# A GeGLU feed-forward kernel on one core: the first token block is transposed by DMA in 128-row slices, all its tiles accumulate at once, and two weight chunks run on it before block two

## The chip, the cores and the metric

The kernel runs on one core of one Trainium2 chip. The metric is device time in microseconds (us), as a median over executions. The profile's span is about 2 us shorter than the device time (590.8 us for a run of 592.9 us).

## The reference

```python
B, S, D, F = 1, 2048, 1024, 3584           # all bf16
def reference(x, w_gate, w_up, w_down):
    return (gelu_tanh(x @ w_gate) * (x @ w_up)) @ w_down
```

The three products are 2688 matmuls of 128x128 weights on 512 columns.

## The kernel before

The 2048 tokens are worked in two halves. A half has two token blocks of 512. Gate and up weights come in seven chunks of 512 columns (1 MB each for gate and up), two chunks in memory at a time. The contraction over D=1024 has eight k-slices of 128. TensorE needs x with D on the partitions (xT), so x must be transposed. Only the start of the first half matters here. Block one comes in two pieces of 512 KB and is transposed by TensorE; three gate and three up tiles (six PSUM banks) accumulate side by side as slices arrive:

```python
    NSU = 3; NWARM = 9; WKP = 2
    load_x0_piece(0, nc.sync)          # xs0[:, :, 0:512], plain load
    load_w0_piece(0, nc.scalar)        # k-slices 0,1 of gate and up, 256 KB each
    ...                                # 9 warm-up matmuls on a constant
    for wp in range(1, NWP):           # the rest of chunk 0, with x piece 1 between
        load_w0_piece(wp, nc.sync)
    for tb in range(1, NTB):           # block two: one 1 MB DMA transpose
        nc.sync.dma_start_transpose(out=xT[:, :, 512:1024], in_=xv[512:1024, :, :])
    chunk_tiles[1] = load_chunk(1)
    # [cut: 7 loads of w_down, 1 MB each]

    def startup_units(hT, wg_sb, wu_sb):
        groups = [transpose_x_piece(0)]          # 16 TensorE transposes + copies
        for kd in range(KD):
            # second transpose_x_piece before kd == 3   [cut]
            g = [mm_gu(su_ps[u][0], wg_sb, xT, u, 0, kd) for u in range(NSU)]
            g += [mm_gu(su_ps[u][1], wu_sb, xT, u, 0, kd) for u in range(NSU)]
    # afterwards: fg (chunk) outer, tb (block) inner
```

The framework that issues the DMAs owns eight completion semaphores for the queues of SP and ACT. It hands them out in the order in which it schedules the DMAs, over both queues. A ninth DMA reuses the first one's semaphore, and its issue waits until that first DMA has landed.

Of the kernel before, what the change touches and what calls it, by code (L numbers as in the profile page):

```python
# [7 lines left out]

ACT = mybir.ActivationFunctionType
ALU = mybir.AluOpType  # L10
BF16 = mybir.dt.bfloat16
# [7 lines left out]
def kernel(  # L19
# [8 lines left out]
    nc = tc.nc  # L28
    P = 128
    x2 = x.flatten_outer_dims()  # L30
# [5 lines left out]
    TB = 512  # L36
# [7 lines left out]
    NDN = D // DN  # L44
    NTS = SH // P
    TSB = TB // P
    XQ = min(512, D)
    NXQ = D // XQ
    KPQ = XQ // P
    WKP = 2 if KD % 2 == 0 else 1  # L50
    NWP = KD // WKP
    NSU = min(3, FPG)
    NWARM = 9

    xv = x2.rearrange("t (ko ki) -> t ko ki", ki=P)
    wgv = w_gate.rearrange("(ko ki) f -> ki ko f", ki=P)
    wuv = w_up.rearrange("(ko ki) f -> ki ko f", ki=P)
    wdv = w_down.rearrange("(ko ki) d -> ki ko d", ki=P)

    const_pool = ctx.enter_context(tc.tile_pool(name="const", bufs=1))  # L60
    xT_pool = ctx.enter_context(tc.tile_pool(name="xT", bufs=1))
    xs_pool = ctx.enter_context(tc.tile_pool(name="xs", bufs=1))
    hT_pool = ctx.enter_context(tc.tile_pool(name="hT", bufs=1))
    wd_pool = ctx.enter_context(tc.tile_pool(name="wd", bufs=1))
    wgu_pool = ctx.enter_context(tc.tile_pool(name="wgu", bufs=2))
    g_pool = ctx.enter_context(tc.tile_pool(name="g", bufs=3))
    o_pool = ctx.enter_context(tc.tile_pool(name="o", bufs=3))
    psum = ctx.enter_context(
        tc.tile_pool(name="psum", bufs=8, space=bass.MemoryType.PSUM)
# [2 lines left out]
    def ps_tile(name):  # L72
        return psum.tile([P, TB], F32, name=name, tag="ps")

    wd_sb = wd_pool.tile([P, KF, D], BF16, name="wd_sb")

    xs0 = xs_pool.tile([P, TSB, D], BF16, name="xs")
    xT = xT_pool.tile([P, KD, SH], BF16, name="xT")
    wg0 = wgu_pool.tile([P, KD, FG], BF16, name="wg_sb")
    wu0 = wgu_pool.tile([P, KD, FG], BF16, name="wu_sb")  # L80

    def load_x0_piece(q, eng):
        eng.dma_start(
            out=xs0[:, :, q * XQ : (q + 1) * XQ],
            in_=x2[0:TB, q * XQ : (q + 1) * XQ].rearrange("(ts p) d -> p ts d", p=P),
        )

    def load_w0_piece(wp, eng):
        k0, k1 = wp * WKP, (wp + 1) * WKP
        eng.dma_start(out=wg0[:, k0:k1, :], in_=wgv[:, k0:k1, 0:FG])  # L90
        eng.dma_start(out=wu0[:, k0:k1, :], in_=wuv[:, k0:k1, 0:FG])

    load_x0_piece(0, nc.sync)
    load_w0_piece(0, nc.scalar)

    nc.scalar.preload_act_table(ACT.Gelu_apprx_tanh)  # L96

    ident = const_pool.tile([P, P], BF16, name="ident")
    make_identity(nc, ident[:])

    warm_insts = []
    if NWARM > 0:
        warm_l = nc.const_aps.tensor(1.0, [P, P], BF16)
        warm_r = nc.const_aps.tensor(1.0, [P, TB], BF16)
        warm_ps = ps_tile("warm_ps")
        for i in range(NWARM):
            warm_insts.append(
                nc.tensor.matmul(  # L108
                    warm_ps[:], lhsT=warm_l, rhs=warm_r, start=True, stop=True
                )  # L110
            )

    x_after = {}
    for q in range(1, NXQ):
        wq = min(max((q * KPQ) // WKP - 1, 0), NWP - 1)
        x_after.setdefault(wq, []).append(q)
    for q in x_after.get(0, []):
        load_x0_piece(q, nc.sync)
    for wp in range(1, NWP):
        load_w0_piece(wp, nc.sync)  # L120
        for q in x_after.get(wp, []):
            load_x0_piece(q, nc.sync)
    for tb in range(1, NTB):
        nc.sync.dma_start_transpose(
            out=xT[:, :, tb * TB : (tb + 1) * TB],
            in_=xv[tb * TB : (tb + 1) * TB, :, :],
        )

    chunk_tiles = {0: (wg0, wu0)}

    def load_chunk(fg):
        wg_sb = wgu_pool.tile([P, KD, FG], BF16, name="wg_sb")
        wu_sb = wgu_pool.tile([P, KD, FG], BF16, name="wu_sb")
        nc.sync.dma_start(out=wg_sb[:], in_=wgv[:, :, fg * FG : (fg + 1) * FG])
        nc.sync.dma_start(out=wu_sb[:], in_=wuv[:, :, fg * FG : (fg + 1) * FG])
        return wg_sb, wu_sb

    if NFG > 1:
        chunk_tiles[1] = load_chunk(1)

    WDP = 4
    for k0 in range(0, KF, WDP):
        k1 = min(KF, k0 + WDP)
        nc.sync.dma_start(out=wd_sb[:, k0:k1, :], in_=wdv[:, k0:k1, :])

    evac_ctr = [0]

    def evac(dst, src):
        if evac_ctr[0] % 2 == 0:
            nc.vector.tensor_copy(out=dst, in_=src)  # L150
        else:
            nc.scalar.copy(out=dst, in_=src)  # L152
        evac_ctr[0] += 1

    def transpose_x_piece(q):
        kds = list(range(q * KPQ, (q + 1) * KPQ))
        banks = []
        if q == 0:
            if TSB % 2 == 0:
                banks.append(([kds[0]], (0, TSB // 2)))  # L160
                banks.append(([kds[0]], (TSB // 2, TSB)))
            else:
                banks.append(([kds[0]], (0, TSB)))
            rest = kds[1:]
            if rest:
                banks.append(([rest[0]], (0, TSB)))
                rest = rest[1:]
        else:
            rest = kds
        for i in range(0, len(rest), 2):  # L170
            banks.append((rest[i : i + 2], (0, TSB)))
        pe_insts = []
        for kd_list, (ts0, ts1) in banks:
            n = (ts1 - ts0) * P
            tp = psum.tile([P, len(kd_list), n], BF16, name="tp", tag="ps")
            for j, kd in enumerate(kd_list):
                for ts in range(ts0, ts1):
                    pe_insts.append(
                        nc.tensor.transpose(  # L179
                            tp[:, j, (ts - ts0) * P : (ts - ts0 + 1) * P],  # L180
                            xs0[:, ts, kd * P : (kd + 1) * P],
                            ident[:],
                        )
                    )
            k0 = kd_list[0]
            evac(xT[:, k0 : k0 + len(kd_list), ts0 * P : ts1 * P], tp[:])
        return pe_insts

    def mm_gu(ps, w_sb, xT_, fi, tb, kd):
        return nc.tensor.matmul(  # L190
            ps[:],
            lhsT=w_sb[:, kd, fi * P : (fi + 1) * P],
            rhs=xT_[:, kd, tb * TB : (tb + 1) * TB],
            start=(kd == 0),
            stop=(kd == KD - 1),
        )

    def unit_tail(hT, gate_ps, up_ps, fc, tb):
        g_sb = g_pool.tile([P, TB], F32, name="g_sb")
        nc.scalar.activation(out=g_sb[:], in_=gate_ps[:], func=ACT.Gelu_apprx_tanh)  # L200
        nc.vector.tensor_tensor(  # L201
            out=hT[:, fc, tb * TB : (tb + 1) * TB],
            in0=g_sb[:],
            in1=up_ps[:],
            op=ALU.mult,
        )

    def unit(hT, xT_, wg_sb, wu_sb, fi, fc, tb):
        gate_ps = ps_tile("gate_ps")
        up_ps = ps_tile("up_ps")  # L210
        for kd in range(KD):
            mm_gu(gate_ps, wg_sb, xT_, fi, tb, kd)
        for kd in range(KD):
            mm_gu(up_ps, wu_sb, xT_, fi, tb, kd)
        unit_tail(hT, gate_ps, up_ps, fc, tb)

    def startup_units(hT, wg_sb, wu_sb):
        groups = [transpose_x_piece(0)]
        su_ps = [(ps_tile("gate_ps"), ps_tile("up_ps")) for _ in range(NSU)]
        for kd in range(KD):  # L220
            for q in range(1, NXQ):
                if kd == q * KPQ - 1:
                    groups.append(transpose_x_piece(q))
            g = [mm_gu(su_ps[u][0], wg_sb, xT, u, 0, kd) for u in range(NSU)]
            g += [mm_gu(su_ps[u][1], wu_sb, xT, u, 0, kd) for u in range(NSU)]
            groups.append(g)
        if warm_insts:
            groups.insert(0, warm_insts)
        for ga, gb in zip(groups[:-1], groups[1:]):
            tc.add_manual_dep(  # L230
                gb[0].ins, ga[-1].ins.name, SCHED_DEP, reason="startup PE order"
            )
        for u in range(NSU):
            unit_tail(hT, su_ps[u][0], su_ps[u][1], u, 0)

    for h in range(NH):
        if h > 0:
            xT = xT_pool.tile([P, KD, SH], BF16, name="xT")
            for tb in range(NTB):
                t0 = h * SH + tb * TB  # L240
                nc.sync.dma_start_transpose(
                    out=xT[:, :, tb * TB : (tb + 1) * TB],
                    in_=xv[t0 : t0 + TB, :, :],
                )
        hT = hT_pool.tile([P, KF, SH], BF16, name="hT")
        for fg in range(NFG):
            if h == 0 and fg in chunk_tiles:
                wg_sb, wu_sb = chunk_tiles[fg]
            else:
                wg_sb, wu_sb = load_chunk(fg)  # L250
            for tb in range(NTB):
                fi_start = 0
                if h == 0 and fg == 0 and tb == 0:
                    startup_units(hT, wg_sb, wu_sb)
                    fi_start = NSU
                for fi in range(fi_start, FPG):
                    fc = fg * FPG + fi
                    unit(hT, xT, wg_sb, wu_sb, fi, fc, tb)
        for ts in range(NTS):
            last = h == NH - 1 and ts == NTS - 1  # L260
            o_sb = o_pool.tile([P, D], BF16, name="o_sb")
# [78 lines left out]
```

## Time and profile before

| what | before | where it is read |
|---|---|---|
| device time, first three runs | 592.93 us (592.72 to 594.9) | run times |
| span; TensorE busy | 590.8 us; 586.4 us (99%) | the page, part 1 |
| eight 512-column matmuls | 1.73 us, 0.216 us each | the chain |
| useful work, 2688 x 0.216 | 580.6 us | worked out |
| first x piece landed; first transpose | 5.42; 5.47 us | the chain |
| first matmul after the startup units | 17.83 us, with 48 useful matmuls done | the timeline |
| useful work starts effectively at | 17.83 - 48 x 0.216 = 7.46 us | worked out |

"Effective start" is the measure used throughout: the time at which the first matmul after the first group begins, less the time that the useful matmuls before it need at full speed. Whatever delays the start is in it once, and the kernel's end moves with it.

From the page of the kernel before, parts 1 and 4:

```profile
span 590.8 us, 6172 instructions
PE 586.4 (99%) x2757; PEld 268.6 (45%) x2757; DVE 78.7 (13%) x116; ACT 88.9 (15%) x148; POOL 0.7 (0%) x6
...
PE 99%; DMA 1%; ACT 0%; issue 0%
```

The chain of waits of its first 20 us (start, duration, what; in these views PE is TensorE, PEld its weight loads, and SPq and ACTq are the DMA queues of SP and ACT):

```profile
0.74 4.69 DMA xs<-in_x_dram
5.42 0.05 issue
5.47 1.07 PE tp L179 x16
6.54 0.65 PE gate_ps L190 x3
7.18 0.03 issue
7.22 0.82 PE up_ps L190 x3
...
10.63 0.89 PE tp L179 x16
...
18.00 1.73 PE gate_ps L190 x8
```

### The profile page before, as it was taken

The numbers are of one execution on the slowest core, as the hardware profiler recorded it, in microseconds if no ns is written. First come the engines' busy times: TensorE is split into PE (matmuls) and PEld (weight loads), VectorE is DVE, ScalarE is ACT, GpSimd is POOL, SyncE is SP. The second block draws the span as 40 slices with busy tenths as digits, with TensorE's granted clock in tenths as the row PEclk, the third lists the DMA queues.
The fourth block names the chain that finished last, engine by engine and source line by source line (L and its number), as shares of the span: only waits on it lengthen the run. The fifth ranks groups of instructions, "written<-read, shape, count | busy, mean of one in ns | idle before, by whom it ended". The sixth has DMA issues, their size and how long they took to land.

```text
span 590.8 us, 6172 instructions
## 1 busy us (share of the span) xinstructions
PE 586.4 (99%) x2757; PEld 268.6 (45%) x2757; DVE 78.7 (13%) x116; ACT 88.9 (15%) x148; POOL 0.7 (0%) x6
## 2 busy tenths in 40 slices
PE   8999999999999999999999999999999999999997
PEld 4444444444444444444444444444444444444445
DVE  0211211121122100000011221121122110000000
ACT  2211112111111110101011112111111110101010
POOL 0000000000000000000000000000000000000000
PEclk9999999999999999999999999999999999999999
DMA  9991404041231480000000413214040000000001
GB/s 273 358 378 59 143 0 143 8 136 52 92 99 44 127 176 19 24 31 18 19 18 3 140 41 103 85 58 131 12 143 1 0 1 0 24 30 19 18 19 36
DMA packets 48969, 45.47 MB, mean 77 GB/s; under 512 B 13360, under 2 KB 43440, under 8 KB 48944
## 3 DMA queue, kind: packets, MB, share of 16 engines
q1 hardware_dynamic: 45952, 40.44, 22.0%
q10 hardware_dynamic: 2992, 4.65, 2.2%
q8 instruction: 21, 0.34, 0.2%
q14 instruction: 4, 0.03, 0.0%
HBM read 37.75 MB, written 4.19 MB: 71 GB/s over the span
## 4 chain that ended last, share of the span: by engine, by line
PE 99%; DMA 1%; ACT 0%; issue 0%
PE up_ps L190 33%; PE gate_ps L190 33%; PE o_ps L295 32%; PE o_ps L271 1%; DMA xs<-in_x_dram 1%; PE tp L179 0%; ACT o_sb L287 0%
## 5 line engine op out<-in xcount | busy, mean ns | idle before, releaser
L190 PE MATMUL up_ps<-xT,wu_sb 128*128 128x512 bf16 x896 | 212.5, 379 | 0.0
L190 PE MATMUL gate_ps<-xT,wg_sb 128*128 128x512 bf16 x896 | 212.5, 379 | 0.0
L295 PE MATMUL o_ps<-wd_sb,hT 128*128 128x512 bf16 x868 | 187.7, 379 | 0.0
L190 PEld LDWEIGHTS <-wu_sb 128*128 128x128 bf16 x896 | 87.6, 98 | 106.0 <-DMA wu_sb<-in_w_up_dram 0.5
L190 PEld LDWEIGHTS <-wg_sb 128*128 128x128 bf16 x896 | 87.6, 98 | 105.2
L295 PEld LDWEIGHTS <-hT 128*128 128x128 bf16 x868 | 84.9, 98 | 102.4
L201 DVE TENSOR_TENSOR hT<-g_sb,up_ps 128x512 bf16<-128x512 f32 x112 | 76.9, 688 | 403.2 <-PE up_ps L190 403.2
L200 ACT ACTIVATE g_sb<-gate_ps 128x512 f32<-128x512 f32 x112 | 66.7, 597 | 312.4 <-PE gate_ps L190 312.4
L302 ACT CAST o_sb<-o_ps 128x512 bf16<-128x512 f32 x31 | 18.2, 586 | 172.6 <-PE o_ps L295 172.6
L279 DVE CAST o_sb<-o_ps 128x256 bf16<-128x256 f32 x1 | 0.4, 425 | 93.0 <-PE o_ps L271 93.0
L271 PE MATMUL o_ps<-wd_sb,hT 128*128 128x256 bf16 x56 | 6.3, 273 | 0.0
L271 PEld LDWEIGHTS <-hT 128*128 128x128 bf16 x56 | 5.5, 98 | 0.9
L108 PE MATMUL warm_ps<-const-bfloat16-1.0 128*128 128x512 bf16 x9 | 4.0, 629 | 0.8 <-PEq L324 0.8
L152 ACT COPY xT<-tp 128x1024 bf16<-128x1024 bf16 (+1 forms) x3 | 2.4, 799 | 7.1 <-PE tp L179 7.1
L179 PE MATMUL tp<-ident,xs 128*128 128x128 bf16 x32 | 2.1, 219 | 0.7 <-DMA xs<-in_x_dram 0.7
L150 DVE COPY xT<-tp 128x256 bf16<-128x256 bf16 (+2 forms) x3 | 1.4, 469 | 10.4 <-PE tp L179 10.4
L179 PEld LDWEIGHTS <-xs 128*128 128x128 bf16 x32 | 1.9, 98 | 1.8 <-DMA xs<-in_x_dram 1.6
L108 PEld LDWEIGHTS <-const-bfloat16-1.0 128*128 128x128 bf16 x9 | 1.2, 141 | 2.7 <-issue 2.7
L96 ACT ACT_TABLE_LOAD x1 | 1.3, 1283 | 1.8 <-issue 1.8
L287 ACT CAST o_sb<-o_ps 128x256 bf16<-128x256 f32 x1 | 0.4, 372 | 5.5 <-PE o_ps L271 5.5
masks.py:199 POOL TENSOR_SCALAR_AFFINE_SELECT ident<-ident 128x128 bf16<-128x128 bf16 x1 | 0.3, 294 | 0.1
masks.py:197 POOL MEMSET ident<- 128x128 bf16 x1 | 0.2, 205 | 0.3 <-POOLq L324 0.3
(4 smaller groups left out, 0.4 us busy)
## 6 DMA issues: line engine op xcount, KB each, us to landing
wg_sb<-in_w_gate_dram SPq DMA_DIRECT2D x13, 1024.0 KB, 5.2
wu_sb<-in_w_up_dram SPq DMA_DIRECT2D x13, 1024.0 KB, 6.8
wd_sb<-in_w_down_dram SPq DMA_DIRECT2D x7, 1024.0 KB, 13.8
out_dram<-o_sb ACTq DMA_DIRECT2D x15, 256.0 KB, 2.0
xs<-in_x_dram SPq DMA_DIRECT2D x2, 512.0 KB, 5.9
wg_sb<-in_w_gate_dram SPq DMA_DIRECT2D x3, 256.0 KB, 6.5
wu_sb<-in_w_up_dram SPq DMA_DIRECT2D x3, 256.0 KB, 6.8
wg_sb<-in_w_gate_dram ACTq DMA_DIRECT2D x1, 256.0 KB, 4.4
```

The source lines that it names most:

```text
L96: nc.scalar.preload_act_table(ACT.Gelu_apprx_tanh)
L108: nc.tensor.matmul(warm_ps[:], lhsT=warm_l, rhs=warm_r, start=True, stop=True)
L150: nc.vector.tensor_copy(out=dst, in_=src)
L152: nc.scalar.copy(out=dst, in_=src)
L179: nc.tensor.transpose(tp[:, j, (ts - ts0) * P : (ts - ts0 + 1) * P], xs0[:, ts, kd * P : (kd + 1) * P], ident[:],)
L190: return nc.tensor.matmul(ps[:], lhsT=w_sb[:, kd, fi * P : (fi + 1) * P], rhs=xT_[:, kd, tb * TB : (tb + 1) * TB], start=(kd == 0), stop=( ...
L200: nc.scalar.activation(out=g_sb[:], in_=gate_ps[:], func=ACT.Gelu_apprx_tanh)
L201: nc.vector.tensor_tensor(out=hT[:, fc, tb * TB : (tb + 1) * TB], in0=g_sb[:], in1=up_ps[:], op=ALU.mult,)
L271: nc.tensor.matmul(o_ps[:, 0:hh], lhsT=hT[:, fc, ts * P : (ts + 1) * P], rhs=wd_sb[:, fc, cc : cc + hh], start=(fc == 0), stop=(fc == KF - 1),
L279: nc.vector.tensor_copy(out=o_sb[:, cc : cc + hh], in_=o_ps[:, 0:hh])
L295: nc.tensor.matmul(o_ps[:], lhsT=hT[:, fc, ts * P : (ts + 1) * P], rhs=wd_sb[:, fc, c0 : c0 + DN], start=(fc == 0), stop=(fc == KF - 1),)
L302: nc.scalar.copy(out=o_sb[:, c0 : c0 + DN], in_=o_ps[:])
```

## The change

The intent is to take the transposes from TensorE, to start on one k-slice instead of four, and to use all eight PSUM banks, so that each slice of x feeds eight matmuls (1.73 us) rather than six. The block order gives TensorE 28 us of work on block one before block two is needed.

```diff
-    NWARM = 9
+    NWARM = 8
-    g_pool = ctx.enter_context(tc.tile_pool(name="g", bufs=3))
+    g_pool = ctx.enter_context(tc.tile_pool(name="g", bufs=4))
-    # [cut: x pieces, identity, TensorE transposes, copies, NSU=3 startup]
+    for kd in range(KD):
+        load_xT(xT, 0, 0, kd, kd + 1)              # 8 DMA transposes on SP
+    for k0, k1 in ((0, 1), (1, 2), (2, 4), (4, 6), (6, 8)):
+        load_w(0, k0, k1, nc.scalar)               # gate and up piece, on ACT
+    # [cut: table load on ACT, 8 warm-up matmuls]
+    load_w(1, 0, KD, nc.sync)                      # chunk 1 ...
+    for tb in range(1, NTB):
+        load_xT(xT, 0, tb, 0, KD)                  # ... then block two
+    def first_block(hT):
+        pairs = [(ps_tile("gate_ps"), ps_tile("up_ps")) for _ in range(FPG)]
+        for kd in range(KD):
+            for fi in range(FPG):
+                for ps, w_sb in zip(pairs[fi], (wg_sb, wu_sb)):
+                    m = mm_gu(ps, w_sb, xT, fi, 0, kd)
+        # [cut: PE order, tails]
+        if h == 0:
+            steps = [(0, 0), (1, 0), (0, 1), (1, 1)] + steps[2 * NTB :]
```

More of the change, by code (lines that the diff above doesn't have):

```diff
@@ L6 @@
 from concourse._compat import with_exitstack
-from concourse.masks import make_identity
 ACT = mybir.ActivationFunctionType
@@ L46 @@
     TSB = TB // P
-    XQ = min(512, D)
-    NXQ = D // XQ
-    KPQ = XQ // P
-    WKP = 2 if KD % 2 == 0 else 1
-    NWP = KD // WKP
-    NSU = min(3, FPG)
-    NWARM = 9
+    NWARM = 8
     xv = x2.rearrange("t (ko ki) -> t ko ki", ki=P)
@@ L58 @@
     wdv = w_down.rearrange("(ko ki) d -> ki ko d", ki=P)
-    const_pool = ctx.enter_context(tc.tile_pool(name="const", bufs=1))
     xT_pool = ctx.enter_context(tc.tile_pool(name="xT", bufs=1))
-    xs_pool = ctx.enter_context(tc.tile_pool(name="xs", bufs=1))
     hT_pool = ctx.enter_context(tc.tile_pool(name="hT", bufs=1))
@@ L75 @@
     wd_sb = wd_pool.tile([P, KF, D], BF16, name="wd_sb")
-    xs0 = xs_pool.tile([P, TSB, D], BF16, name="xs")
     xT = xT_pool.tile([P, KD, SH], BF16, name="xT")
-    wg0 = wgu_pool.tile([P, KD, FG], BF16, name="wg_sb")
-    wu0 = wgu_pool.tile([P, KD, FG], BF16, name="wu_sb")
-    def load_x0_piece(q, eng):
-        eng.dma_start(
-            out=xs0[:, :, q * XQ : (q + 1) * XQ],
-            in_=x2[0:TB, q * XQ : (q + 1) * XQ].rearrange("(ts p) d -> p ts d", p=P),
-        )
-    def load_w0_piece(wp, eng):
-        k0, k1 = wp * WKP, (wp + 1) * WKP
-        eng.dma_start(out=wg0[:, k0:k1, :], in_=wgv[:, k0:k1, 0:FG])
-        eng.dma_start(out=wu0[:, k0:k1, :], in_=wuv[:, k0:k1, 0:FG])
@@ L93 @@
-    load_x0_piece(0, nc.sync)
-    load_w0_piece(0, nc.scalar)
-    nc.scalar.preload_act_table(ACT.Gelu_apprx_tanh)
-    ident = const_pool.tile([P, P], BF16, name="ident")
-    make_identity(nc, ident[:])
-    warm_insts = []
-    if NWARM > 0:
-        warm_l = nc.const_aps.tensor(1.0, [P, P], BF16)
-        warm_r = nc.const_aps.tensor(1.0, [P, TB], BF16)
-        warm_ps = ps_tile("warm_ps")
-        for i in range(NWARM):
-            warm_insts.append(
-                nc.tensor.matmul(
-                    warm_ps[:], lhsT=warm_l, rhs=warm_r, start=True, stop=True
-                )
-            )
@@ L113 @@
-    x_after = {}
-    for q in range(1, NXQ):
-        wq = min(max((q * KPQ) // WKP - 1, 0), NWP - 1)
-        x_after.setdefault(wq, []).append(q)
-    for q in x_after.get(0, []):
-        load_x0_piece(q, nc.sync)
-    for wp in range(1, NWP):
-        load_w0_piece(wp, nc.sync)
-        for q in x_after.get(wp, []):
-            load_x0_piece(q, nc.sync)
-    for tb in range(1, NTB):
-        nc.sync.dma_start_transpose(
-            out=xT[:, :, tb * TB : (tb + 1) * TB],
-            in_=xv[tb * TB : (tb + 1) * TB, :, :],
-        )
@@ L129, with new_chunk @@
-    chunk_tiles = {0: (wg0, wu0)}
-    def load_chunk(fg):
+    chunks = {}
+    def new_chunk(fg):
         wg_sb = wgu_pool.tile([P, KD, FG], BF16, name="wg_sb")
         wu_sb = wgu_pool.tile([P, KD, FG], BF16, name="wu_sb")
-        nc.sync.dma_start(out=wg_sb[:], in_=wgv[:, :, fg * FG : (fg + 1) * FG])
-        nc.sync.dma_start(out=wu_sb[:], in_=wuv[:, :, fg * FG : (fg + 1) * FG])
-        return wg_sb, wu_sb
-    if NFG > 1:
-        chunk_tiles[1] = load_chunk(1)
+        chunks[fg] = (wg_sb, wu_sb)
+        return chunks[fg]
@@ new lines, in load_w, with load_xT @@
+    def load_w(fg, k0, k1, eng):
+        wg_sb, wu_sb = chunks[fg]
+        c0, c1 = fg * FG, (fg + 1) * FG
+        eng.dma_start(out=wg_sb[:, k0:k1, :], in_=wgv[:, k0:k1, c0:c1])
+        eng.dma_start(out=wu_sb[:, k0:k1, :], in_=wuv[:, k0:k1, c0:c1])
+    def load_xT(xT_, h, tb, k0, k1):
+        t0 = h * SH + tb * TB
+        nc.sync.dma_start_transpose(
+            out=xT_[:, k0:k1, tb * TB : (tb + 1) * TB],
+            in_=xv[t0 : t0 + TB, k0:k1, :],
+        )
+    new_chunk(0)
+    for kd in range(KD):
+        load_xT(xT, 0, 0, kd, kd + 1)
@@ new lines @@
+    for k0, k1 in ((0, 1), (1, 2), (2, 4), (4, 6), (6, 8)):
+        load_w(0, k0, k1, nc.scalar)
+    nc.scalar.preload_act_table(ACT.Gelu_apprx_tanh)
+    warm = []
+    warm_l = nc.const_aps.tensor(1.0, [P, P], BF16)
+    warm_r = nc.const_aps.tensor(1.0, [P, TB], BF16)
+    warm_ps = ps_tile("warm_ps")
+    for i in range(NWARM):
+        warm.append(
+            nc.tensor.matmul(
+                warm_ps[:], lhsT=warm_l, rhs=warm_r, start=True, stop=True
+            )
+        )
+    new_chunk(1)
@@ L141 @@
+    load_w(1, 0, KD, nc.sync)
+    for tb in range(1, NTB):
+        load_xT(xT, 0, tb, 0, KD)
     WDP = 4
     for k0 in range(0, KF, WDP):
-        k1 = min(KF, k0 + WDP)
-        nc.sync.dma_start(out=wd_sb[:, k0:k1, :], in_=wdv[:, k0:k1, :])
-    evac_ctr = [0]
-    def evac(dst, src):
-        if evac_ctr[0] % 2 == 0:
-            nc.vector.tensor_copy(out=dst, in_=src)
-        else:
-            nc.scalar.copy(out=dst, in_=src)
-        evac_ctr[0] += 1
-    def transpose_x_piece(q):
-        kds = list(range(q * KPQ, (q + 1) * KPQ))
-        banks = []
-        if q == 0:
-            if TSB % 2 == 0:
-                banks.append(([kds[0]], (0, TSB // 2)))
-                banks.append(([kds[0]], (TSB // 2, TSB)))
-            else:
-                banks.append(([kds[0]], (0, TSB)))
-            rest = kds[1:]
-            if rest:
-                banks.append(([rest[0]], (0, TSB)))
-                rest = rest[1:]
-        else:
-            rest = kds
-        for i in range(0, len(rest), 2):
-            banks.append((rest[i : i + 2], (0, TSB)))
-        pe_insts = []
-        for kd_list, (ts0, ts1) in banks:
-            n = (ts1 - ts0) * P
-            tp = psum.tile([P, len(kd_list), n], BF16, name="tp", tag="ps")
-            for j, kd in enumerate(kd_list):
-                for ts in range(ts0, ts1):
-                    pe_insts.append(
-                        nc.tensor.transpose(
-                            tp[:, j, (ts - ts0) * P : (ts - ts0 + 1) * P],
-                            xs0[:, ts, kd * P : (kd + 1) * P],
-                            ident[:],
-                        )
-                    )
-            k0 = kd_list[0]
-            evac(xT[:, k0 : k0 + len(kd_list), ts0 * P : ts1 * P], tp[:])
-        return pe_insts
@@ L189, in mm_gu @@
+        nc.sync.dma_start(out=wd_sb[:, k0 : k0 + WDP, :], in_=wdv[:, k0 : k0 + WDP, :])
     def mm_gu(ps, w_sb, xT_, fi, tb, kd):
@@ L206, in unit_tail, with unit @@
         )
-    def unit(hT, xT_, wg_sb, wu_sb, fi, fc, tb):
+    def unit(hT, xT_, fg, fi, tb):
+        wg_sb, wu_sb = chunks[fg]
         gate_ps = ps_tile("gate_ps")
@@ L214, in unit @@
             mm_gu(up_ps, wu_sb, xT_, fi, tb, kd)
-        unit_tail(hT, gate_ps, up_ps, fc, tb)
-    def startup_units(hT, wg_sb, wu_sb):
-        groups = [transpose_x_piece(0)]
-        su_ps = [(ps_tile("gate_ps"), ps_tile("up_ps")) for _ in range(NSU)]
-        for kd in range(KD):
-            for q in range(1, NXQ):
-                if kd == q * KPQ - 1:
-                    groups.append(transpose_x_piece(q))
-            g = [mm_gu(su_ps[u][0], wg_sb, xT, u, 0, kd) for u in range(NSU)]
-            g += [mm_gu(su_ps[u][1], wu_sb, xT, u, 0, kd) for u in range(NSU)]
-            groups.append(g)
-        if warm_insts:
-            groups.insert(0, warm_insts)
-        for ga, gb in zip(groups[:-1], groups[1:]):
-            tc.add_manual_dep(
-                gb[0].ins, ga[-1].ins.name, SCHED_DEP, reason="startup PE order"
-            )
-        for u in range(NSU):
-            unit_tail(hT, su_ps[u][0], su_ps[u][1], u, 0)
+        unit_tail(hT, gate_ps, up_ps, fg * FPG + fi, tb)
+    def first_block(hT):
+        wg_sb, wu_sb = chunks[0]
+        pairs = [(ps_tile("gate_ps"), ps_tile("up_ps")) for _ in range(FPG)]
+        last = warm[-1]
+        for kd in range(KD):
+            for fi in range(FPG):
+                for ps, w_sb in zip(pairs[fi], (wg_sb, wu_sb)):
+                    m = mm_gu(ps, w_sb, xT, fi, 0, kd)
+                    tc.add_manual_dep(
+                        m.ins, last.ins.name, SCHED_DEP, reason="startup PE order"
+                    )
+                    last = m
+        for fi in range(FPG):
+            unit_tail(hT, pairs[fi][0], pairs[fi][1], fi, 0)
     for h in range(NH):
@@ L239 @@
             for tb in range(NTB):
-                t0 = h * SH + tb * TB
-                nc.sync.dma_start_transpose(
-                    out=xT[:, :, tb * TB : (tb + 1) * TB],
-                    in_=xv[t0 : t0 + TB, :, :],
-                )
-        hT = hT_pool.tile([P, KF, SH], BF16, name="hT")
-        for fg in range(NFG):
-            if h == 0 and fg in chunk_tiles:
-                wg_sb, wu_sb = chunk_tiles[fg]
-            else:
-                wg_sb, wu_sb = load_chunk(fg)
-            for tb in range(NTB):
-                fi_start = 0
-                if h == 0 and fg == 0 and tb == 0:
-                    startup_units(hT, wg_sb, wu_sb)
-                    fi_start = NSU
-                for fi in range(fi_start, FPG):
-                    fc = fg * FPG + fi
-                    unit(hT, xT, wg_sb, wu_sb, fi, fc, tb)
+                load_xT(xT, h, tb, 0, KD)
+        hT = hT_pool.tile([P, KF, SH], BF16, name="hT")
+        steps = [(fg, tb) for fg in range(NFG) for tb in range(NTB)]
+        if h == 0:
+            steps = [(0, 0), (1, 0), (0, 1), (1, 1)] + steps[2 * NTB :]
+        else:
+            chunks.clear()
+        for fg, tb in steps:
+            if fg not in chunks:
+                new_chunk(fg)
+                load_w(fg, 0, KD, nc.sync)
+            if h == 0 and fg == 0 and tb == 0:
+                first_block(hT)
+                continue
+            for fi in range(FPG):
+                unit(hT, xT, fg, fi, tb)
         for ts in range(NTS):
```

## The prediction

> **What bounds the kernel now.** On the page of the kernel before, TensorE is busy 586.4 of 590.8 us; the chain of waits is 99% TensorE, at full clock. Eight 512-column matmuls take 1.73 us in the chain (0.216 us each), and the useful work equals 2688 of them: 580.6 us. So about 10.2 us is not useful work. The timeline places it: about 2.9 us at the end (last matmul done near 587.9, then copy and store); the rest at the start. The first matmul after the startup units begins at 17.83 us with 48 useful matmuls done (10.37 us), so the start has lost 7.46 us: 0.74 us before any instruction, warm-up matmuls and the wait for the first x piece until 5.46, two batches of sixteen TensorE transposes (about 0.9 us of issue each), and some 0.9 us waiting for the first copy and the first up weights (landed 7.15).
>
> **What the change does.** It removes both transpose batches, their six copies and the identity. The first token block comes through eight 128 KB DMA transposes from SP, while ACT issues the first weight chunk in smaller first pieces. Each k-slice feeds 8 matmuls (1.73 us) instead of 6 (1.30), so TensorE starts after about 384 KB instead of 768 KB and tolerates slower arrivals. Chunk 1 gets a deadline near 18.5 us; block two is deferred to about 32 us. Later work is the same; when eight banks are released at once, the 0.6 us gelu and 0.69 us multiply keep up.
>
> **Costs from the trace.** A 1 MB DMA transpose occupied the SP queue 4.9 to 6.6 us and landed 7.3 to 10.3 us after its issue: 0.6 to 0.85 us of issue per slice, below the 1.73 us that TensorE needs. The last part lands about 2.3 us after issue ends, so I estimate slice 0 at 3.7 to 4.4 us, and the first gate and up pieces at 4 to 4.9 us (before: 256 KB landed at 5.14 beside 512 KB of x). The first block needs 3 MB; mixed with transposes the DMA moved 240 to 290 GB/s, so it is done near 13 us; the last slice is needed near 17 us. The Trainium skill, "DMA: Bandwidth & Descriptors", Latency and other measured facts, states 261 GB/s for a DMA transpose with a non-contiguous middle dimension; this trace's 200 to 260 GB/s roughly agrees. By the instruction order, DMAs share eight completion semaphores, so later pieces wait for an earlier landing (weights for slices 2 and 3 wait for x slices 0 and 2). I allow 0.3 to 1 us of stalls for that and for a matmul or two at the slow clock (0.43 us).
>
> **Prediction.** Useful work starts effectively at about 5.0 us (4.4 to 6.5) instead of 7.46. The whole gain is on the critical path, because TensorE never waits afterwards: about 2.4 us, 0.4%. Time 590.5 us, range 589.2 to 592.7. Faster by over 2%: 0.01; within 2%: 0.98; slower: 0.01.
>
> **What would show each step.** Timeline: first real matmul at 4 to 5 us; first unit of chunk 1 beginning near 18.8 us against an equivalent 21.3 before; SP transpose issues of 0.6 to 0.85 us. Waits: TensorE idle on DMA under 1 us in total after its first real matmul, none for chunk 1 or PSUM. The kernel's end unchanged.
>
> **What would make it wrong.** A fixed cost of 2 us or more per small DMA transpose, or the semaphore chain spacing slices over 1.73 us apart, would stall every step and eat the gain (up to some us slower). Chunk 1, competing with the last pieces, could land after 18.5 us. TensorE still at the slow clock when data comes would cost 0.2 us per matmul.

## The result and the profile after

| | before | after |
|---|---|---|
| median | 593.9 us (592.72 to 594.9, 4 runs) | 595.35 us (593.92 to 595.84, 4 runs) |
| span of the profiled run | 590.8 us | 593.4 us |
| first real matmul | 6.37 us | 4.86 us |
| first matmul after the first group | 17.83 us (48 done) | 23.59 us (64 done) |
| effective start | 7.46 us | 9.77 us |

The ratio of after to before is 1.0023, 95% interval 0.9998 to 1.0047. Ratios here are the mean time of one kernel's fast runs over that of the other's of the same rounds, so not quite the ratio of the medians quoted. By the 2% rule the two are the same; the predicted gain of 2.4 us is absent. Two of the four runs of the kernel before were of its slower group (see e6); against the other two (592.72 and 592.93 us) all four runs of the changed kernel are slower, by about 1 us or more. In the profiles the start lost 2.3 us more (9.77 - 7.46) where it should have lost 2.4 us less, and the span is 2.6 us longer.

From the page after, parts 1 and 4:

```profile
span 593.4 us, 6100 instructions
PE 584.4 (98%) x2724; PEld 266.6 (45%) x2724; DVE 77.1 (13%) x113; ACT 86.3 (15%) x145; POOL 0.2 (0%) x4
...
PE 96%; DMA 2%; SPq 1%; issue 0%; ACT 0%
```

TensorE does 2.0 us less and the span grows: the profile has a new wait. The DMA waits of TensorE and of its weight loads in the first 30 us (waiting engine and line, releaser: total us, times, longest):

```profile
PEld L116 <- DMA wu_sb<-in_w_up_dram: 6.1, 4, 3.0
PE up_ps L116 <- DMA wu_sb<-in_w_up_dram: 3.9, 2, 2.7
...
PE gate_ps L116 <- DMA xT<-in_x_dram: 0.7, 1, 0.7
PEld L116 <- DMA wg_sb<-in_w_gate_dram: 0.7, 1, 0.7
...
PE gate_ps L116 <- DMA wg_sb<-in_w_gate_dram: 0.2, 1, 0.2
```

The matmuls' waits for up weights are two long ones. Taken from the starts of successive matmuls, the losses after the first are 0.30 us (slice 1), 0.38 and 2.88 us (slice 2, gate then up), and 1.34 us (slice 6, up): 4.9 us. The chain of waits shows what held the last of those up weights back:

```profile
0.73 1.24 SPq L84
1.97 0.06 issue
2.03 1.24 SPq L84
...
5.92 1.26 SPq L84
7.17 0.04 issue
7.22 5.63 DMA xT<-in_x_dram
12.85 0.02 issue
12.87 7.43 DMA wu_sb<-in_w_up_dram
20.29 0.05 issue
20.34 0.39 PE up_ps L116
```

Read from the top: SP issues one slice each 1.3 us; the sixth slice (issue 7.22) lands at 12.85; only then, at 12.87, does ACT issue the last up piece, which lands at 20.29. An x slice and an up piece have no data in common. They share a completion semaphore. The same holds at slice 2: ACT's sixth DMA (up weights of slices 2 and 3) waited for the third x slice. ACT's queue in the timeline (start, duration, issue):

```profile
0.73 0.38 ACTq L79 DMA_DIRECT2D wg_sb<-in_w_gate_dram  x1
...
2.10 0.60 ACTq L80 DMA_DIRECT2D wu_sb<-in_w_up_dram  x1
4.83 0.39 ACTq L79 DMA_DIRECT2D wg_sb<-in_w_gate_dram  x1
7.45 0.38 ACTq L80 DMA_DIRECT2D wu_sb<-in_w_up_dram  x1
9.34 0.38 ACTq L79 DMA_DIRECT2D wg_sb<-in_w_gate_dram  x1
...
12.87 0.38 ACTq L80 DMA_DIRECT2D wu_sb<-in_w_up_dram  x1
```

The gaps from 2.70 to 4.83, 5.22 to 7.45, 7.83 to 9.34 and 10.76 to 12.87 us are ACT standing in line for x slices 0, 2, 3 and 5, which landed at 4.81, 7.43, 9.31 and 12.85 us. The piece of 7.45 landed at 12.04, and TensorE went on at 12.09.

### The profile page after: what moved, and what is told of

Read it like the earlier page. It is cut to its first block, busy times and chain, and to the rows that moved or that the text cites. A ratio compares the mean times of both kernels' runs of the same rounds, so it can differ in the third digit from the quotient of the medians.

```text
span 593.4 us, 6100 instructions
## 1 busy us (share of the span) xinstructions
PE 584.4 (98%) x2724; PEld 266.6 (45%) x2724; DVE 77.1 (13%) x113; ACT 86.3 (15%) x145; POOL 0.2 (0%) x4
## 3 DMA queue, kind: packets, MB, share of 16 engines
HBM read 36.70 MB, written 4.19 MB: 69 GB/s over the span
## 4 chain that ended last, share of the span: by engine, by line
PE 96%; DMA 2%; SPq 1%; issue 0%; ACT 0%
PE up_ps L116 32%; PE gate_ps L116 32%; PE o_ps L215 32%; DMA wu_sb<-in_w_up_dram 1%; SPq L84 1%; PE o_ps L191 1%; DMA xT<-in_x_dram 1%; ACT o_sb L207 0%
## 5 line engine op out<-in xcount | busy, mean ns | idle before, releaser
L116 PE MATMUL up_ps<-xT,wu_sb 128*128 128x512 bf16 x896 | 216.2, 379 | 3.9 <-DMA wu_sb<-in_w_up_dram 3.9
L116 PE MATMUL gate_ps<-xT,wg_sb 128*128 128x512 bf16 x896 | 216.2, 379 | 1.1 <-DMA xT<-in_x_dram 0.7
```

What stands on the lines that cost most here:

```text
L116: return nc.tensor.matmul(ps[:], lhsT=w_sb[:, kd, fi * P : (fi + 1) * P], rhs=xT_[:, kd, tb * TB : (tb + 1) * TB], start=(kd == 0), stop=( ...
```

## The experiments

Three theories were on the table. **A**: weight pieces are issued late because they share completion semaphores with x slices. **B**: the DMA transposes themselves are slow, in issue or in transfer. **C**: the new block order asks for chunk 1 too early, and its 2 MB compete with the last pieces. A fourth question came up from the two groups into which the kernel before's times fall.

| run | edit | this, median (range) | ratio to before, 95% interval | effective start in the profile |
|---|---|---|---|---|
| after | the change | 595.35 (593.92 to 595.84) | 1.0023 (0.9998 to 1.0047) | 9.77 |
| e1 | semaphore order fixed | 592.32 (591.78 to 592.66) | 0.9976 (0.9953 to 1.0000) | 6.1 |
| e2 | old block and load order | 596.99 (594.78 to 598.34) | 1.0049 (1.0018 to 1.0081) | 12.2 |
| e3 | two slices per transpose | 593.94 (592.97 to 594.41) | 1.0000 (0.9978 to 1.0022) | 8.8 |
| e4 | later transposes in slices | 594.52, one look | none | 9.1 |
| e5 | e1, x loaded plainly (wrong result) | 592.19, one look | none | 6.8 |
| e6 | kernel before again | 595.25, one look | none | 9.75 |
| e7 | e1 with finer weight pieces | 591.84 (591.16 to 592.77) | 0.9975 (0.9960 to 0.9991) | 5.7 |
| e8 | before with finer pieces | 592.7 (592.51 to 592.95) | 0.9988 (0.9973 to 1.0003) | 7.0 |
| e9 | before, 11 warm-ups | 593.08 (592.99 to 593.21) | 0.9991 (0.9978 to 1.0004) | not used |
| e10 | e7, 10 warm-ups | 592.32 (591.74 to 593.14) | 0.9977 (0.9961 to 0.9992) | not used |
| e11 | e9 repeated | 593.29 (593.11 to 593.31) | 0.9996 (0.9982 to 1.0010) | not used |
| e12 | before with the new block order | 592.98 (592.93 to 594.51) | 0.9999 (0.9977 to 1.0022) | not used |

In the traces of e1 to e4 one matmul record of the first block is missing (63 records for 64 matmuls); the missing one is counted here. By the 2% rule every run with a ratio is the same as the kernel before. The ratios mix that kernel's two groups of times (see e6), so the explanation rests on the waits in the profiles.

### e1: the same DMAs, numbered so that kinds do not mix

```diff
+    # order only, no waits: weight piece, x slice, weight piece, x slice, ...
+    order = [ws_[0], xs_[0], ws_[1], xs_[1], ..., ws_[7], xs_[7], ws_[8], c1_[0], ws_[9], c1_[1], t1_, act_, *wd_]
+    for a, b in zip(order[:-1], order[1:]):
+        tc.add_manual_dep(b.ins, a.ins.name, SCHED_DEP, reason="startup DMA order")
```

With kinds alternating over eight semaphores, a weight piece reuses a weight piece's semaphore and an x slice an x slice's. Sizes, queues and the order within each queue are those of the changed kernel.

> The changed kernel with the same DMAs, sizes and queues; only the order in which the DMAs are numbered is fixed, so that a weight piece reuses the completion semaphore of an earlier weight piece and an x slice that of an earlier x slice. Theory A (weight pieces issued late because they wait for x slices): TensorE waits for up weights of 3.0 us at slice 2 and 1.7 us at slice 6 shrink to under 1 us together, the first block ends near 19.5 us instead of 23.4 us. Theory B (the DMA transposes are slow and nothing else matters): x slices still land as late, TensorE waits for x in their place, the first block ends near 23 us. Theory C (chunk 1 is asked for too early): the first block ends early, but TensorE then waits 1 to 3 us for chunk 1, which still lands at 20 and 23 us, and the span gains at most 2 us. I expect A with part of C: span 590.5 to 592.

Measured: the first block ends at 20.0 us instead of 23.6, the span is 589.7 us. ACT's queue, sixth and tenth DMA:

```profile
3.98 0.41 ACTq L81 DMA_DIRECT2D wu_sb<-in_w_up_dram  x1
...
9.37 0.38 ACTq L81 DMA_DIRECT2D wu_sb<-in_w_up_dram  x1
```

These were issued at 7.45 and 12.87 us in the changed kernel. The DMA waits of TensorE that are left in the first 30 us:

```profile
PEld L126 <- DMA wu_sb<-in_w_up_dram: 1.4, 2, 1.1
PE gate_ps L126 <- DMA xT<-in_x_dram: 0.8, 1, 0.8
```

No matmul waits for up weights any more. What is left is one wait, a loss of 0.93 us at slice 2, for x this time: the third slice now landed at 9.56 us (7.43 in the changed kernel), probably because the weights no longer stand back for it, and its up weights at 9.35 us, only just before. Chunk 1 landed at 18.2 and 21.2 us, in time. Theory A holds: nothing but the numbering was changed, and it is worth 3.6 us in the profiles and 3.0 us in the medians. The two kernels did not run in the same rounds, but e4, which starts like the changed kernel, took 594.52 us in e1's job, where the four runs of e1 took 591.78 to 592.66 us. Two differences between the profiles need not come from the numbering, and they work against each other: the first x slice landed at 4.15 us instead of 4.81 (4.68 in e7, 5.35 in e10), and TensorE was at its slow clock until 6.3 us (see e6), which cost about 1.0 us.

### e2: the old block and load order

```diff
-    load_w(1, 0, KD, nc.sync)
     for tb in range(1, NTB):
         load_xT(xT, 0, tb, 0, KD)
+    load_w(1, 0, KD, nc.sync)
-            steps = [(0, 0), (1, 0), (0, 1), (1, 1)] + steps[2 * NTB :]
```

> The changed kernel with the block order and the load order of the kernel before (block two transposed ahead of chunk 1, then block two on chunk 0). Theory C: the last up piece, which took 7.4 us to land beside chunk 1, lands about 2 us earlier, and the span falls by 1 to 2 us. Theory A: the 3.0 us wait at slice 2 is unchanged, the span changes by under 1.5 us; a new wait for block two is possible since its transpose is issued at 11 us and lands near 20 us. Expected span 592 to 594.

Measured: slower in the median, against what every theory expected (the range overlaps that of the changed kernel). The last up piece took 9.36 us to land (13.35 to 22.71) rather than 7.43: beside a 1 MB DMA transpose it fared worse than beside chunk 1. The wait at slice 2 stayed (2.14 us). So C falls as the main cause. e1 says it more plainly: there chunk 1 was issued only 1 us later than in the changed kernel (12.18 against 11.13 us), and no matmul waited for an up piece. C keeps a part: the last up piece, issued at 9.37 us in e1, took 4.57 us to land, and 7.43 us when it was issued late, with chunk 1 already under way.

### e3: two slices per DMA transpose

```diff
-    for kd in range(KD):
-        load_xT(xT, 0, 0, kd, kd + 1)
+    for kd in range(0, KD, 2):
+        load_xT(xT, 0, 0, kd, kd + 2)
```

> The changed kernel with the first block in four DMA transposes of two slices (256 KB) instead of eight of one. Theory B in the form that every DMA transpose instruction has a fixed cost: a two-slice issue takes about 1.8 us, not 2.5 us, all four are issued by about 7.5 us instead of 11.1 us, the last x lands near 11 us instead of 13 to 14 us. The first matmul moves from 4.9 to about 5.5 us. The numbering also changes (only one early weight piece waits for an x slice), so theory A expects the 3.0 us wait to shrink here too; run e1 tells the two apart. First block ends at 19.5 to 21.5 us; span 590.5 to 592.5.

Measured: the first two-slice issues took 1.33 and 1.28 us, hardly more than one slice's 1.24, so at these sizes the cost is nearly all per instruction. But the third and fourth took 1.93 and 4.06 us, the last x landed at 15.69 us rather than 11, and small weight pieces behind the bigger transposes took 6.9 us to land (second up piece, 2.12 to 9.04). TensorE lost 1.90 us at slice 1 and 1.39 us at slice 2. The last up piece still shared a semaphore with an x piece and was issued at 11.54 us. It gained little: fewer issues did not help here, where the third and fourth issue and the landings became longer.

### e4: single slices where the DMA is quiet

```diff
             for tb in range(NTB):
-                load_xT(xT, h, tb, 0, KD)
+                for kd in range(KD):
+                    load_xT(xT, h, tb, kd, kd + 1)
```

> The changed kernel with the second half's two transposes, off the critical path near 203 us, also cut into single slices, where the DMA is quiet. It measures the cost of one slice by itself. Fixed cost per instruction: each issue again takes about 1.2 us (against 4.7 us for eight slices in one instruction, 0.6 us each), so sixteen take about 20 us. If instead the 1.24 us at the start came from contention with the weights: 0.6 to 0.7 us each, about 10 us in all. Total time unchanged from the changed kernel.

SP's queue in the timeline near 203 us, first in the changed kernel, then in e4:

```profile
203.35 9.41 SPq L84 DMA_TRANSPOSE xT<-in_x_dram  x2
```

```profile
202.66 21.00 SPq L84 DMA_TRANSPOSE xT<-in_x_dram  x16
```

The same 2 MB cost 9.41 us of issue in two instructions and 21.00 us in sixteen: 4.7 us for eight slices against 1.31 us for one. The 1.24 us at the start is thus a cost of each instruction, not contention. My 0.6 to 0.85 us had come from dividing a long transpose by eight.

### e5: the same bytes without transposing

```diff
-        return nc.sync.dma_start_transpose(out=xT_[:, k0:k1, ...], in_=xv[t0 : t0 + TB, k0:k1, :])
+        if k1 - k0 == 1:   # numbers wrong on purpose
+            return nc.sync.dma_start(out=xT_[:, k0, ...], in_=x2[t0 : t0 + P, ...])   # 128 KB
```

> Run e1's kernel with the eight DMA transposes of the first block replaced by plain loads of the same 128 KB each (so the result is wrong on purpose). Same queues, same numbering. It measures what the transposing itself costs once the semaphore order is fixed. Theory B (256-byte packets and 1.24 us issues of the transposes are the remaining limit): issues fall to about 0.45 us, the slice that landed 6.2 us after its issue lands in about 4 us, TensorE never waits over 0.3 us after its first matmul, and useful work is delayed only by the first arrival (about 4 us) and any matmuls at the slow clock: first block ends near 18.0 to 18.7 us against 20.0 in e1. If the limit is just the 3 MB of bytes, the 0.9 us wait at slice 2 stays.

Measured: issues of x fell to 0.33 to 0.43 us, the third slice landed at 5.58 us instead of 9.56. Yet TensorE still lost 1.13 us at slice 2, now for up weights (issued 4.42, landed 10.04):

```profile
PE up_ps L131 <- DMA wu_sb<-in_w_up_dram: 1.0, 1, 1.0
```

The first block ended at 20.6 us, no earlier than in e1. So faster x alone does not bring the end forward: with pieces of 256 KB queued for both gate and up, slice 2 was late with and without transposing. This is one look, and it does not rule out theory B as the limit that is left once the numbering is right: with short issues SP also reached chunk 1 at 6.83 us instead of 12.18, so chunk 1 was under way beside the up weights of slice 2. A run with chunk 1 held back was not made. With the original numbering B keeps a part too, which these runs do not separate: slow landings of x slices are what the chain passes on to the weights.

### e7 and e10: finer weight pieces

```diff
-    for k0, k1 in ((0, 1), (1, 2), (2, 4), (4, 6), (6, 8)):
+    for k0, k1 in ((0, 1), (1, 2), (2, 3), (3, 4), (4, 6), (6, 8)):
+    # and e1's alternating order
```

> Run e1's kernel with weight pieces of one slice for slices 0 to 3 (128 KB) and two slices after that, in the same alternating order. If TensorE waited 0.9 us at slice 2 in e1 because 256 KB weight pieces were queued ahead of x, that wait falls under 0.4 us, and the first block ends 0.5 to 1 us earlier than in e1 at equal clock; span 589 to 589.7. If the mix of transposes and weights is simply too slow, the wait moves to slice 3 or 4 and nothing is gained.

Measured: after its first matmul TensorE waits once, for chunk 1:

```profile
PE up_ps L126 <- DMA wu_sb<-in_w_up_dram: 0.4, 1, 0.4
PE gate_ps L126 <- DMA xT<-in_x_dram: 0.4, 1, 0.4
```

The second line is the first x slice (first real matmul 4.73 us); the first is chunk 1's up half, which landed at 21.74 us and cost 0.56 us by the starts of the matmuls. The first block ended at 19.5 us with no wait inside. This beats both kernels, though by far less than the 2% of the rule: the ratio to the kernel before is 0.9975, interval 0.9960 to 0.9991; the median is 3.5 us under the changed kernel's (other rounds, ranges apart) and about 1.1 us under the median of the eight lower-group runs of the kernel before in the same job (592.77 to 593.09 us). Against e1 the medians differ by 0.5 us with overlapping ranges, so the finer pieces are shown by the profile's waits, not by the times.

In e10 this kernel got two more warm-up matmuls (10 instead of 8).

> Run e7's kernel with 10 warm-up matmuls instead of 8, filling the 0.8 us before the first x slice lands at 4.7 us. The warm-up then ends at about 5.0 us, 0.3 us too late, but TensorE is never idle before the clock rises. Expected within 0.3 us of e7 in the median (591.5 to 592.1), with less spread at the top (e7: 591.2 to 592.8). If the idle stretch does not matter here: 0.2 to 0.3 us slower.

Measured: 592.32 us, range 591.74 to 593.14, no tighter than e7. Its profile had waits of its own, one of 1.01 us for chunk 1. It settles nothing; e7 keeps the lowest median.

### e8: finer pieces in the kernel before

```diff
-    XQ = min(512, D)
+    XQ = min(256, D)
-    WKP = 2 if KD % 2 == 0 else 1
+    WKP = 1
```

> The kernel before, with x in four pieces of 256 KB instead of two of 512 KB and weight pieces of one slice instead of two; still transposed by TensorE. Tests whether smaller first pieces, and not the DMA transposes, are what shortens the start. First x lands near 4.2 us instead of 5.4, first up piece near 4.5 instead of 7.2; the start loses about 6.3 us instead of 7.5: span about 589.7 and time 591.8 in the lower group. If waits between its 24 pieces on 8 semaphores hold it up, TensorE waits over 1 us in total for weights after the first matmul and nothing is gained.

Measured: the first x landed at 4.49 us, the first up piece at 4.99, and no wait for weights followed. The effective start came down only to 7.0 us instead of the 6.3 I had expected, and the span to 590.4. All four runs (592.51 to 592.95 us) lie in the kernel before's lower group or just under it. Finer pieces alone, with TensorE still transposing, are worth some 0.4 us in the profile, which the ratio (0.9988, interval up to 1.0003) does not separate from nothing.

### e6, e9, e11: two groups of times in the kernel before

Over all jobs, and without the single look of e6, 29 of 44 runs of the kernel before took 592.7 to 593.3 us and 15 took 594.5 to 595.1; none lie between. My prediction started from a profile of the lower group.

> The kernel before, unchanged. Its times fall in two groups, 592.7 to 593.0 and 594.6 to 595.0 us. If TensorE's slow clock at the start explains it, a profile from the upper group shows the 16 transposes and the first matmuls after 5.4 us still at 0.43 us spacing until 6.5 to 7.6 us, and the matmul after the startup units begins near 19.7 us instead of 17.8. If DMA timing explains it, x or weights land later instead. If this run falls in the lower group it shows 17.8 us again and settles nothing.

This fell in the upper group (595.25 us, span 593.1). Its chain:

```profile
0.74 5.15 DMA xs<-in_x_dram
5.88 0.05 issue
5.93 1.89 PE tp L179 x16
7.82 1.28 PE gate_ps L190 x3
9.10 1.22 PE up_ps L190 x3
10.32 0.65 PE gate_ps L190 x3
```

The x piece landed 0.46 us later than in the first profile. But sixteen transposes took 1.89 us instead of 1.07, and three matmuls 1.28 instead of 0.65: TensorE ran at half speed until 10.1 us. The clock column shows 1.00 all the same, so on the page this is only seen in the matmuls' spacing (0.43 against 0.216 us). The reason lies in the kept traces: their clock record begins only at the turn to fast, and time before it counts as full speed. The Trainium skill, "TensorE: Matmul & The Clock Gate", part 1, says that the fast clock comes after a busy window of about 3.4 us and that windows run freely, whatever the kernel does. The traces agree with that as far as they go: of the thirteen that have a clock record, twelve turn between 3.77 us (the changed kernel) and 6.69 us (e7), and this one at 10.13 us. In this, TensorE sat idle for about 1.2 us before the first x (4.77 to 5.93 us), between the warm-up and the transposes. Reckoned back from the turn with the page's 3.4 us (an estimate), that idle stretch fell inside the window before the last one, which may be why that window did not release the clock. The test was to fill the stretch:

```diff
-    NWARM = 9
+    NWARM = 11
```

> The kernel before with 11 warm-up matmuls instead of 9, so that TensorE is busy until 5.4 us, when the first x lands, instead of idle from 4.6 to 5.4 or 5.9 us. If the two groups of times (592.9 and 594.7) come from TensorE staying slow until about 10 us because of that idle stretch, the upper group disappears or moves to about 593.5; the lower group stays at 592.8 to 593.0. If the groups come from DMA timing, both stay.

> The same kernel as e9, to see whether six of six in the lower group was luck: over all jobs 12 of 33 runs of the kernel before lie in the upper group. If the idle stretch is the cause, all six are again between 592.8 and 593.6 us. If not, about two of the six lie near 594.7. A profile in which TensorE is still slow at 5.6 us would show it turn fast near 6.6 us rather than near 10 us.

Measured: 592.99 to 593.21 us in e9 and 593.11 to 593.31 us in e11: twelve of twelve in the lower group. With 29 of 44 otherwise, that would happen by chance about seven times in a thousand; with the 16 of 22 of the same two jobs, about two times in a hundred. The ratios (0.9991 and 0.9996, intervals across 1) do not separate the means. The profile of e11 has x landing as late as e6's (5.87 us), with TensorE at full speed:

```profile
0.74 5.13 DMA xs<-in_x_dram
5.87 0.05 issue
5.91 1.07 PE tp L179 x16
6.98 0.65 PE gate_ps L190 x3
```

Its span is 591.1 us against 593.1 in e6. So in the one profile of the upper group the slow clock, and not DMA timing, makes most of the difference, and the idle stretch is its probable cause. Neither profile of the 11 warm-ups caught a late turn, so the exact condition stays open.

### e12: the new block order in the kernel before

```diff
+        if h == 0:
+            steps = [(0, 0), (1, 0), (0, 1), (1, 1)] + steps[2 * NTB :]
+    # and chunk 1 loaded ahead of block two's transpose
```

> The kernel before with only the changed block order: two weight chunks on block one, then block two, chunk 1 loaded ahead of block two's transpose. It isolates the third part of the change. If the order alone costs or gains nothing, as I predicted: within 0.5 us of the kernel before in the same group, the matmul after the startup units still at 17.8 or 20.1 us, no TensorE wait over 0.3 us after it. If the earlier deadline for chunk 1 (21.3 us) is too early even without DMA transposes in the first block, a wait for it appears after 21 us and the time rises by as much.

Measured: 592.98 us, ratio 0.9999 (one of the four runs, 594.51 us, fell in the upper group); TensorE waits for nothing after its first x; chunk 1 landed at 15.5 and 19.8 us. The order by itself is neutral, as predicted.

## Why the prediction was wrong

**Right.** The bound (TensorE, 99% of the chain) and the place of the loss (the start). No wait for PSUM. The block order is neutral by itself (e12). All the later work is the same; the end took 3.2 us after its last copy began, against 2.9.

**Right by luck.** The first real matmul: 4 to 5 us predicted, 4.86 measured. But the x slice that it waited for landed at 4.81 us, later than the 3.7 to 4.4 that I had estimated, and its weights landed earlier (2.97 and 3.87 us) than the 4 to 4.9. No wait for chunk 1: it landed at 20.1 and 23.1 us and was used from 23.6. At the 18.8 us that I had forecast for its first use it would have been late; e7, whose first block ended at 19.5 us, did wait for it.

**Wrong, and the step that failed.** "I allow 0.3 to 1 us of stalls for that and for a matmul or two at the slow clock." The stalls were 4.9 us, so "TensorE never waits afterwards" was false and the whole gain was lost. The mechanism had been named, eight shared completion semaphores and weights for slices 2 and 3 waiting for x slices 0 and 2; it was mis-sized, for two terms that feed it were wrong:

- "0.6 to 0.85 us of issue per slice" measured 1.24 us, a cost per instruction (e4: 1.31 us even in quiet).
- "The last part lands about 2.3 us after issue ends" measured 2.9 us for the third slice (4.56 to 7.43) and 4.4 us for the sixth (8.48 to 12.85). In e4's quiet stretch 11 of 16 slices landed 1.3 to 1.6 us after their issue ended, so the weights in flight beside them are the likely reason.

In a chain those errors add up: the third slice landed at 7.43 us (three issues of 0.6 to 0.85 us and 2.3 us would have made it about 4.8 to 5.6), and only then was a piece issued that took another 4.6 us. The sixth landed at 12.85, followed by 7.4 us. So "it is done near 13 us" became 20.29 us. I had weighed the bytes (3 MB at 240 to 290 GB/s) as if all were queued early. The same kernel with the numbering fixed (e1) loses 0.93 us to waits and about 1.0 us to the slow clock, together still more than the allowance for both; from a first matmul at 4.19 us it reaches an effective start of 6.1 us, inside the 4.4 to 6.5 us that I gave.

**Also missed.** The baseline has two groups, 2 us apart, as large as the gain sought. The first three runs had shown it (592.72, 592.93, 594.9), and I treated it as noise.

**Left open.** What transposing costs once the numbering is right and chunk 1 is held back; how much of the late x landings is the transposing and how much the mere bytes, under the original numbering; what exactly keeps the clock low; and what sets the scatter of the changed kernel (593.92 to 595.84 us).

## What to carry to other kernels

Cutting a transfer into more DMAs is not free when completion semaphores are few: list which earlier landing each DMA's issue waits for, and make sure that a DMA on the critical path never reuses the semaphore of a slow or unrelated one; here a change of order alone was worth 3 us. Cost a DMA from one of its own size, not from a fraction of a larger one, and add latencies along the chain of waits before comparing bytes with bandwidth. Before chasing 2 us, look at the spread of the baseline: here one changed number, which filled TensorE's idle stretch ahead of the first data, left no run of twelve in the slow group.

## What the Trainium skill lacked or had wrong

- "DMA: Bandwidth & Descriptors", Why a DMA increments its semaphore by 16 and not by 1, advises one semaphore per in-flight transfer, but no page says what a small ring of them costs: the issue of a later DMA waits for a landing on another queue. Here ACT stood 2.1 to 2.2 us three times and 1.5 us once, and TensorE lost 4.9 us, against 0.93 us of waits once the order was changed (e1).
- The same page gives a bandwidth for DMA transposes (261 GB/s with a non-contiguous middle dimension) but no trn2 issue time by size. The runs show 1.12 to 1.27 us for most slices of 128 KB (1.31 us from one to the next in e4), 1.28 and 1.33 us for the first two of 256 KB in e3, and 4.7 us for 1 MB in quiet. At that pace of issue 1 MB per 4.7 us is about 223 GB/s (an estimate), somewhat under the page's figure.
- "TensorE: Matmul & The Clock Gate", part 1, puts the warm-up at under 1% of a typical span and advises not to fit to a specific count of slow matmuls. The size agrees: the two groups here are 0.3% apart (592.9 and 594.7 us). But that is close to the 0.4% gain that was sought, and with two more warm-up matmuls none of 12 runs fell in the upper group. No page says that a clock record can begin only at the turn to fast, so that a mean over it reads 1.00 while matmuls run at half speed (0.43 us spacing in e6, turn at 10.13 us).
